# Retention and FFN on one core: output copies that step on the other side, last states on ScalarE, one q on GpSimd

## The chip, the core and the metric

The kernel runs on one core of a Trainium2 chip. The core has a matrix engine (TensorE, PE in the profile; its weight loads are shown apart as PEld), VectorE (DVE), ScalarE (ACT), GpSimd (POOL) and SyncE (SP), which here only starts DMAs. Each engine works through its own instructions in order. Products land in PSUM, which ACT and DVE read; everything else lies in SBUF. The metric is the device time of one execution in microseconds.

## What is computed

The reference is a retention layer (attention without a softmax, with a decay per head) whose output goes through a two-layer FFN with ELU. Eight batches, eight heads, 576 tokens, 64 values a head; the FFN goes from 512 to 2048 and back.

```
scores = q @ k^T / sqrt(64)                      # per batch and head, 576 x 576
gamma  = 1 - 2 ** (-5 - head)
ret    = scores * (gamma ** (i - j) if i >= j else 0)
x      = (ret @ v), heads side by side           # 4608 tokens x 512
h      = x @ w_in                                # 512 -> 2048
g      = h if h > 0 else exp(h) - 1
out    = g @ w_out                               # 2048 -> 512, float32
```

## The kernel before

The decay is separable, so q is scaled by gamma to the power of the token's position and k by its inverse (lines 224 to 235). Retention then runs in chunks: products within a chunk under a triangular mask, and a running state (the sum of k times v so far) that earlier chunks hand on.

The work is cut into **units**. Unit u is a batch b, a half T of the first 512 tokens and a half w of the heads; four units make a batch, so units 0 to 3 are the first batch and units 4 to 11 the next two (from batch 3 on, "fine" units of another shape are used). The last 64 tokens of each batch, the "riders", are worked off beside later units. For every unit the kernel

- scales and casts q and k and casts v (`cast`, with a letter per operand for the engine: v is VectorE, s ScalarE, p GpSimd),
- turns q and k over (on PE with `turn_pe` or `turn0`, later by a transposing DMA with `turn`),
- makes scores (`scores`), masks them on DVE (`masks`), multiplies them with v (`values`) and adds what earlier chunks contribute (`inter`),
- makes its own state (`state`), which DVE adds into running sums (`prefix_mid`, `prefix_end`); `put_mid` and `put_end` copy these as bf16 to where PE reads them. For the second half of a batch `put_end` calls `put_last`, which fills `s_last`; only the batch's rider reads that,
- copies the unit's output from PSUM into `xt`, the FFN's input (`put_x`, lines 392 to 403).

Tokens do not lie in order. A load gives each partition two neighbouring tokens (four for q of the first batch), so that the columns of a unit's output in PSUM come as e groups of r columns, e being 4 in the first batch and 2 in units 4 to 11. In `xt` the tokens are in order, so that the token with number r*e + i comes from column i*n + r, n being the columns of a group. `put_x` undoes this while it copies, one copy of 128 x 256 for each of the two PSUM banks `x0` and `x1`. Unit 3 is copied in two parts of 128 x 128 a bank, one of the four on DVE. Fine units copy without a step on line 398. The two banks hold one unit's output at a time: the products of the next unit must wait until the copies have read them.

The FFN's first layer (`ffn1`, and `ffn1_half` for half a batch's tokens) multiplies `xt` with `w_in`; ELU takes two ACT instructions (lines 639 and 642) and one DVE instruction (line 643); the second layer (`ffn2`) multiplies with `w_out`, and ACT copies the result for the store (line 686).

The order of all instructions on each engine is written out by hand at the end of the kernel: first the first batch's attention (lines 788 to 883), in which the weights are also loaded and cast; the FFN of the first batch with units 4 to 7 between (lines 911 to 1004); then stages that mix the FFN of one batch with the attention of the next. The loads wait in SP's queue in the order of lines 788 to 797 and 911 to 917. Products of the first FFN columns (`part`) are interleaved with unit 3's attention (lines 863 to 883). Within the span that the change touches, the order is

```
    cast(4, "p", "p", None)
    cast_w(14)
    cast_w(15)
    put_end(2)
    put_end(3)
    half1 = f1h(1, 0)
```

then a part of the second layer, the turn of unit 4 on PE, `cast_v(4, "s")`, the casts of unit 5 (line 961), more of the second layer, and `stretch(4, "p")`, which makes unit 4's scores and state and, for later units, also finishes the unit before.

Of the kernel before, what the change touches and what calls it, by code (L numbers as in the profile page):

```python
# [17 lines left out]
def kernel(  # L18
# [15 lines left out]
    P = 128  # L34
# [130 lines left out]
    def weights(k):  # L165
        for h in range(2 * (k < 2)):

            r, c = slice(2 * h * P, 2 * (h + 1) * P), slice(k * 2 * P, (k + 1) * 2 * P)
            yield h, moe_w_in[r, c].rearrange("(j p) c -> p j c", j=2), w_in_sb[:, 2 * h : 2 * h + 2, c]
        for i in (2 * k, 2 * k + 1) if k > 1 else ():  # L170
            n, j = divmod(i, KJ)
            if n < KJ:
                c = slice(n * 512, (n + 1) * 512)
                yield i % 2, moe_w_in[j * P : (j + 1) * P, c], w_in_sb[:, j, c]
            else:
                f = i - KJ * KJ
                yield i % 2, moe_w_out[f * P : (f + 1) * P, :], w_out_sb[:, f, :]

    def load_w(k):
        staged[k] = raw.tile([P, 2, 4, 2, D], FP32, name="rqk", tag="rqk").rearrange("p i h e d -> p i (h e d)")  # L180
        for h, src, dst in weights(k):
            pin(nc.sync.dma_start(staged[k][:, h] if k > 1 else staged[k][:, h].rearrange("p (j c) -> p j c", j=2), src))
# [12 lines left out]
    def fine(u):  # L195
        return seq[u][0] >= 3
# [5 lines left out]
    xps, begun = [None, None], set()  # L202

    def load(u, last=False):
        b, T, w = seq[u]
        rqk = raw.tile([P, 2, 4, 2, D], FP32, name="rqk", tag="rqk")
        rv = raw.tile([P, 4, 2, D], FP32, name="rv", tag="rv", bufs=5)
        parts = [(rqk[:, 0], q), (rqk[:, 1], k), (rv, v)]
        if fine(u):
            t = u % 4  # L210
            for dst, src in parts:
                pin(nc.sync.dma_start(
                    dst.rearrange("p a e d -> p (a e) d"), src[b, :, t * P : (t + 1) * P, :].rearrange("h p d -> p h d"),
                ))
            rawt[u] = rqk, rv
            return
        for dst, src in parts[::-1] if last else parts:
            pin(nc.sync.dma_start(
                dst.rearrange("p h e d -> p h (e d)"),
                src[b, 4 * w : 4 * w + 4, 2 * P * T : 2 * P * (T + 1), :].rearrange("h (p e) d -> p h (e d)", e=2),  # L220
            ))
        rawt[u] = rqk, rv

    def cast_qk(u, i, eng, es=(0, 1)):
        b, T, w = seq[u]
        if fine(u):
            pin(tt[eng](  # L227
                natt[u][0][:, i].rearrange("p e h d -> p (e h) d"), rawt[u][0][:, i].rearrange("p a e d -> p (a e) d"),
                (gqf, gkf)[i][:, u % 4].unsqueeze(2).to_broadcast([P, H, D]), ALU.mult,
            ))  # L230
            return
        x = rawt[u][0][:, i].rearrange("p h e d -> p e h d")
        g = (gq, gk)[i][:, 2 * T : 2 * T + 2, 4 * w : 4 * w + 4].unsqueeze(3).to_broadcast([P, 2, 4, D])
        for e in es:
            pin(tt[eng](natt[u][0][:, i, e], x[:, e], g[:, e], ALU.mult))

    def cast_v(u, eng):
        pin(engines[eng](natt[u][1], rawt[u][1]))  # L238

    def cast(u, q="p", k="p", v="p"):  # L240
        if u >= NS:
            return
        qkn = nat.tile([P, 2, 2, 4, D], BF16, name="qkn", tag="qkn")
        vn = nat.tile([P, 4, 2, D], BF16, name="vn", tag="vn", bufs=5)
        natt[u] = qkn, vn
        if q:
            cast_qk(u, 0, q)
        if k:
            cast_qk(u, 1, k)
        if v:  # L250
            cast_v(u, v)
# [43 lines left out]
    def new_x():  # L295
        for c in range(2):
            xps[c] = ps_x.tile([P, 512], FP32, name="x", tag=f"x{c}")
        begun.clear()
# [60 lines left out]
    def inter(u, hls=(0, 1), to=None):  # L359
        b, T, w = seq[u]  # L360
        x = to or xps
        if fine(u):
            for m, i, c in fines:
                if u % 4 + c:
                    r = half(c)
                    q = trt[u][r, m, r] if i == c else swapped[u][r, m]
                    acc_x(c, i, x[c][half(i), m * C : (m + 1) * C], s_fine[u % 2][r, m, i], q)
            return
        for c in range(2):
            if T + c == 0:  # L370
                continue
            s = s_mid[w] if c else s_first[w]
            for hl in hls:
                acc_x(c, 2, grouped(u, x[c][:, hl * P : (hl + 1) * P]), s[:, hl], queries(u, slice(0, P), hl, c), to)
# [17 lines left out]
    def put_x(u, hls=(0, 1), to=None, eng="ss"):  # L392
        b, T, w = seq[u]
        h0, h1 = hls[0], hls[-1] + 1
        for c in range(2):
            if fine(u):
                o = w * P + c * C
                pin(engines[eng[c]](xt_tile(b)[:, T, :, o : o + C], xps[c][:, : HP * C].rearrange("p (m n) -> p m n", m=HP)))  # L398
                continue
            e = 2 if u >= FT else 4  # L400
            src = (to or xps)[c][:, : 2 * P].rearrange("p (h e r) -> p h e r", h=2, e=e)[:, h0:h1]
            dst = xt_tile(b)[:, T, 2 * w + h0 : 2 * w + h1, c * P : (c + 1) * P].rearrange("p h (r e) -> p h e r", e=e)
            pin(engines[eng[c]](dst, src))  # L403

    def drop(u):
# [80 lines left out]
    def blocks(dst, src, eng):  # L486
        for i in range(2):
            pin(engines[eng](dst[half(i), :, half(i)], src[half(i)]))  # L488

    def put_last(b, w, src, eng):  # L490
        for i in range(2):
            pin(engines[eng](s_last[b % 3][half(w), :, i], src[half(i)]))
# [4 lines left out]
    def put_end(u, eng="p"):  # L497
        b, T, w = seq[u]
        if T:
            put_last(b, w, total[w], eng)  # L500
        else:
            blocks(s_first[w], total[w], eng)
# [32 lines left out]
    def scores_rider(b):  # L535
        for m, c, i in quads:
            t = trr[b][half(i), 2 * c + m]
            acc_x(i, c, beside(i, m, half(c)), t[:, ST:], t[:, :ST])
# [14 lines left out]
    def inter_rider(b):  # L553
        for m, c, i in quads:
            r = half(c)
            q = trr[b][r, 2 * c + m, :ST] if i == c else swapped[b, "r"][r, m]
            acc_x(c, i, beside(c, m, half(i)), s_last[b % 3][r, m, i], q)

    def values_rider(b):
        for m, c, i in quads:  # L560
            acc_x(c, i, beside(c, m, half(i)), natr[b][1][half(c), 2 * m + i], ptr[b][half(c), i, m])
# [9 lines left out]
    def stretch(u, put="p", end="p"):  # L571
        old = u - 1 in natt and u - 1 in ptt
        rider = late.pop() if late else None
        new_x()
        if rider is not None:
            inter_rider(rider)
        if old:
            inter(u - 1)
        if u < NS:
            scores(u)  # L580
            if fine(u):
                state(u)
            masks(u)
        if u in rides:
            scores_rider(rides[u])
        if old:
            values(u - 1)
        if rider is not None:
            values_rider(rider)
        if u < NS and not fine(u):  # L590
            state(u)
        if old:
            put_x(u - 1)
            drop(u - 1)
        if rider is not None:
            put_rider(rider)
        if u < NS:
            if fine(u):
                prefix_fine(u)
            else:  # L600
                prefix_mid(u, put)
                prefix_end(u, end)
        if u in rides:
            masks_rider(rides[u])
            late.append(rides[u])
# [16 lines left out]
    def xt_tile(g):  # L622
        if g == B:
            return xtail
        if g not in xts:
            xts[g] = xpool.tile([P, 2, KJ, 2 * P], BF16, name="xt", tag="xt")
        return xts[g]
# [283 lines left out]
    for kk in (4, 5, 10, 11, 6, 7, 12, 13):  # L911
        load_w(kk)
    load(4)
    for kk in (14, 15):
        load_w(kk)
    for u in range(5, 10):
        load(u)
    F = {0: {}, 1: dict(pool=ps_h, tag="ph"), 2: dict(pool=ps_h, tag="ph"), 3: {}}

    def row(ft):  # L920
# [22 lines left out]
    cast(4, "p", "p", None)  # L943
    cast_w(14)
    cast_w(15)
    put_end(2)
    put_end(3)
    half1 = f1h(1, 0)

    def some():  # L950
# [7 lines left out]
    quad(0)  # L958
    turn_pe(4, "vs", pool=ps_x, tags=("x0", "x1"))
    cast_v(4, "s")  # L960
    cast(5, "v", "p", None)
    quad(1)
    quad(2)
    stretch(4, "p")
# [5 lines left out]
    cast_v(5, "s")  # L970
    cast(6, "v", "p", None)
    quad(3)
    stretch(5, end=None)
    quad(4)
    turn_pe(6, "vs")
    cast_v(6, "s")
    cast(7, "v", "p", None)
    put_end(5)
    turn(7)
    load(10)  # L980
    quad(5)
# [77 lines left out]
    c = [j for g, hf in twos[E:] for j in f2(g, (2 * hf, 2 * hf + 1))]  # L1059
# [56 lines left out]
```

## Time and profile before

| | us |
|---|---|
| median of 3 runs | 303.45 (303.23 to 303.67) |
| profiled execution, whole | 304.17 |
| its span on the core | 302.2 |
| PE busy | 290.1 |
| ACT busy | 213.0 |
| DVE busy | 176.4 |
| POOL busy | 175.1 |

The granted clock of PE was at full speed throughout. In the rows that follow, a row of the timeline gives start and duration in microseconds, the engine, the line of the kernel, the operation, the tile written and the tiles read with their shapes, how many such instructions the row merges, and in brackets how long the engine stood idle before it and whose end released it. A row of a line's summary gives the smallest, median and largest duration in nanoseconds, then the first and last start. A row of a table by stretches gives the stretch, its length, the busy time and number of products, the granted clock, the DMA share and GB/s.

### The profile page before, as it was taken

The numbers are of one execution on the slowest core, as the hardware profiler recorded it, in microseconds if no ns is written. First come the engines' busy times: TensorE is split into PE (matmuls) and PEld (weight loads), VectorE is DVE, ScalarE is ACT, GpSimd is POOL, SyncE is SP. The second block draws the span as 40 slices with busy tenths as digits, with TensorE's granted clock in tenths as the row PEclk, the third lists the DMA queues.
The fourth block names the chain that finished last, engine by engine and source line by source line (L and its number), as shares of the span: only waits on it lengthen the run. The fifth ranks groups of instructions, "written<-read, shape, count | busy, mean of one in ns | idle before, by whom it ended". The sixth has DMA issues, their size and how long they took to land.

```text
span 302.2 us, 9051 instructions
## 1 busy us (share of the span) xinstructions
PE 290.1 (96%) x3591; PEld 176.5 (58%) x3628; DVE 176.4 (58%) x353; ACT 213.0 (70%) x433; POOL 175.1 (58%) x346
## 2 busy tenths in 40 slices
PE   8789999999999999999999999999999999999995
PEld 5444446776776666666767765554445444456654
DVE  5656568755555666756686765758675734332210
ACT  5679847976767776777777787777777776764531
POOL 7589887687957585868496887468852300011000
PEclk9999999999999999999999999999999999999999
DMA  6999999999999999999799999999761000001112
GB/s 202 316 370 356 346 304 280 227 217 172 248 177 219 169 216 235 206 207 186 191 196 215 184 199 206 202 242 177 172 90 38 37 35 36 37 35 69 37 69 69
DMA packets 132394, 54.33 MB, mean 180 GB/s; under 512 B 107712, under 2 KB 126400, under 8 KB 132352
## 3 DMA queue, kind: packets, MB, share of 16 engines
q1 hardware_dynamic: 129600, 45.04, 74.0%
q0 software_dynamic: 2672, 8.65, 8.6%
q8 instruction: 28, 0.46, 0.7%
q14 instruction: 14, 0.11, 0.1%
q10 hardware_dynamic: 80, 0.07, 0.1%
HBM read 36.70 MB, written 9.44 MB: 153 GB/s over the span
## 4 chain that ended last, share of the span: by engine, by line
PE 89%; DMA 2%; ACT 2%; issue 2%; SPq 1%; POOL 1%; DVE 1%; DVEq 0%; POOLq 0%
PE ph L65 40%; PE pm L65 39%; PE x L65 4%; PE sc L65 3%; DMA rqk<-in_k_dram 2%; PE pe L65 1%; ACT ph L642 1%; POOL s_pair L488 1%; ACT e L639 1%; SPq L731 1%; SPq L717 1%; PE ptr L269 0%; POOL qkn L750 0%; DVE pt L348 0%; DVE pt L354 0%
## 5 line engine op out<-in xcount | busy, mean ns | idle before, releaser
L643 DVE SCALAR_TENSOR_TENSOR g<-e,ph 128x512 bf16<-128x512 f32 x128 | 86.4, 686 | 84.6 <-ACT ph L642 81.2
L65 PE MATMUL ph<-xt,w_in_sb 128*128 128x256 bf16 (+1 forms) x768 | 128.7, 308 | 0.5 <-ACT xt L403 0.3
L65 PE MATMUL pm<-w_out_sb,g 128*128 128x512 bf16 x478 | 123.8, 379 | 3.1 <-issue 2.1
L639 ACT ACTIVATE e<-ph 128x512 f32<-128x512 f32 x144 | 86.0, 597 | 52.8 <-PE ph L65 51.0
L65 PEld LDWEIGHTS <-w_in_sb 128*128 128x128 bf16 x896 | 86.4, 98 | 50.7 <-issue 0.9
L642 ACT ACTIVATE ph<-ph 128x512 f32<-128x512 f32 x144 | 83.8, 591 | 0.0
L65 PEld LDWEIGHTS <-g 128*128 128x128 bf16 x512 | 48.6, 98 | 43.9 <-issue 0.2
L696 POOL DMA_DIRECT2D out_dram<-ot x35 | 19.9, 569 | 44.6 <-ACT ot L686 44.2
L468 POOL CAST s_fine<-run 64x256 bf16<-64x256 f32 x40 | 15.9, 396 | 42.4 <-DVE run L437 33.5
L686 ACT COPY ot<-pm 128x512 f32<-128x512 f32 x35 | 20.5, 588 | 14.9 <-PE pm L65 14.8
L643 DVE SCALAR_TENSOR_TENSOR gt<-e,ph 128x512 bf16<-128x512 f32 x16 | 10.9, 686 | 18.8 <-ACT ph L642 17.2
L227 POOL TENSOR_TENSOR qkn<-rqk,gqf 128x512 bf16<-128x512 f32 x20 | 21.1, 1053 | 0.4
L227 POOL TENSOR_TENSOR qkn<-rqk,gkf 128x512 bf16<-128x512 f32 x20 | 20.9, 1046 | 0.0
L65 PE MATMUL ph<-xtail,w_in_sb 128*128 128x256 bf16 x128 | 16.4, 273 | 0.0
L398 ACT CAST xt<-x 128x256 bf16<-128x256 f32 x40 | 12.9, 378 | 5.0 <-PE x L65 5.0
L437 DVE TENSOR_TENSOR run<-sc,run 128x256 f32<-128x256 f32 x35 | 14.9, 425 | 1.2
L238 POOL CAST vn<-rv 128x512 bf16<-128x512 f32 x24 | 14.6, 608 | 1.5
L341 DVE TENSOR_TENSOR pt<-sc,mask_t 128x512 bf16<-128x512 f32 x20 | 13.7, 684 | 0.0
L488 POOL CAST s_pair<-mid 64x128 bf16<-64x128 f32 x24 | 7.0, 292 | 11.4 <-DVE mid L437 6.6
L474 POOL CAST s_fine<-run 64x256 bf16<-64x256 f32 x30 | 11.9, 395 | 1.8
L459 DVE COPY qs<-qkT 64x256 bf16<-64x256 bf16 x40 | 12.0, 300 | 0.6
L65 PE MATMUL sc<-qkT 64*64 64x64 bf16 (+1 forms) x512 | 11.6, 204 | 0.5 <-ACT qkT L760 0.4
(106 smaller groups left out, 270.2 us busy)
## 6 DMA issues: line engine op xcount, KB each, us to landing
rqk<-in_q_dram SPq DMA_DIRECT2D x32, 256.0 KB, 4.3
rqk<-in_k_dram SPq DMA_DIRECT2D x32, 256.0 KB, 5.4
rv<-in_v_dram SPq DMA_DIRECT2D x32, 256.0 KB, 5.5
out_dram<-ot POOLq DMA_DIRECT2D x31, 256.0 KB, 3.4
rqk<-in_moe_w_in_dram SPq DMA_DIRECT2D x16, 256.0 KB, 5.7
rqk<-in_moe_w_out_dram SPq DMA_DIRECT2D x16, 256.0 KB, 5.9
rqt<-in_q_dram SPq DMA_DIRECT2D x8, 128.0 KB, 5.2
rqt<-in_k_dram SPq DMA_DIRECT2D x8, 128.0 KB, 4.5
```

Of the source, the lines that this page charges most:

```text
L65: pin(nc.tensor.matmul(*a, **kw))
L227: pin(tt[eng](natt[u][0][:, i].rearrange("p e h d -> p (e h) d"), rawt[u][0][:, i].rearrange("p a e d -> p (a e) d"), (gqf, gkf)[i][:, u % ...
L238: pin(engines[eng](natt[u][1], rawt[u][1]))
L341: pin(nc.vector.tensor_tensor(ptt[u], sc[:, :, : HP * C].rearrange("p i (m n) -> p i m n", m=HP), mask_t.unsqueeze(1).unsqueeze(1).to_broa ...
L398: pin(engines[eng[c]](xt_tile(b)[:, T, :, o : o + C], xps[c][:, : HP * C].rearrange("p (m n) -> p m n", m=HP)))
L437: pin(nc.vector.tensor_tensor(dst, a, b, ALU.add))
L468: pin(nc.gpsimd.tensor_copy(s_fine[u % 2][half(1), :, i], new[half(i), 0]))
L639: pin(nc.scalar.activation(e, ph, AF.Exp))
L642: pin(nc.scalar.activation(ph, ph, AF.Relu))
L643: pin(nc.vector.scalar_tensor_tensor(dst, view(e), -1.0, view(ph), ALU.add, ALU.min))
L686: pin(nc.scalar.copy(ot, pm))
L696: pin((queue or nc.gpsimd).dma_start(dst, src))
```

## The change

`put_x` reads its two sides in another order: the access pattern's inner dimension is now the group e, so that the written tokens lie side by side and the read of PSUM steps from group to group. This holds for units 0 to 11, whatever e is; fine units are untouched. `put_end(2)` and `put_end(3)` go from GpSimd to ScalarE and stand behind the cast of unit 4's v. The scaling of q of unit 5, the sixth unit, goes from VectorE to GpSimd, where the scaling of its k already was. The other lines spell out loops and default arguments and issue the same instructions in the same order.

```diff
@@ put_x
             e = 2 if u >= FT else 4
-            src = (to or xps)[c][:, : 2 * P].rearrange("p (h e r) -> p h e r", h=2, e=e)[:, h0:h1]
-            dst = xt_tile(b)[:, T, 2 * w + h0 : 2 * w + h1, c * P : (c + 1) * P].rearrange("p h (r e) -> p h e r", e=e)
+
+            src = (to or xps)[c][:, : 2 * P].rearrange("p (h e r) -> p h r e", h=2, e=e)[:, h0:h1]
+            dst = xt_tile(b)[:, T, 2 * w + h0 : 2 * w + h1, c * P : (c + 1) * P].rearrange("p h (r e) -> p h r e", e=e)
             pin(engines[eng[c]](dst, src))
@@ loads behind the first batch
-    for kk in (14, 15):
-        load_w(kk)
-    for u in range(5, 10):
-        load(u)
+    load_w(14)
+    load_w(15)
+    load(5)
+    load(6)
+    load(7)
+    load(8)
+    load(9)
@@ the first batch's FFN
     cast_w(14)
     cast_w(15)
-    put_end(2)
-    put_end(3)
     half1 = f1h(1, 0)
@@
     cast_v(4, "s")
-    cast(5, "v", "p", None)
+    put_end(2, "s")
+    put_end(3, "s")
+    cast(5, "p", "p", None)
     quad(1)
@@
-    stretch(5, end=None)
+    stretch(5, "p", end=None)
@@
-    put_end(5)
+    put_end(5, "p")
```

## The prediction

> **What bounds the kernel now.** I read the page first, then the busy time of TensorE (PE) by stretch, then the timeline of each engine around the copies that the diff touches.
>
> ```profile
> PE 290.1 (96%) x3591; PEld 176.5 (58%) x3628; DVE 176.4 (58%) x353; ACT 213.0 (70%) x433; POOL 175.1 (58%) x346
> ...
> PE 89%; DMA 2%; ACT 2%; issue 2%; SPq 1%; POOL 1%; DVE 1%; DVEq 0%; POOLq 0%
> ```
> ```profile
> 14.00:20.88 6.88, 5.40 (x150) 1.00 1.05 365
> 20.88:50.00 29.12, 28.79 (x250) 1.00 1.07 330
> ```
> PE bounds it: 96% busy, 89% of the chain that ended last. From 20.88 us on it runs almost without a gap; before, while the first batch's attention is worked off, it idles 1.48 of 6.88 us. So a change is worth what it moves of the moment at which PE starts its dense part, plus or minus new gaps later. What PE waited for ahead of 20.88:
>
> ```profile
> 15.98 0.27 PE L65 MATMUL x<-qkT,s_pair 128*128 128x128 bf16 x2 [0.39 <-POOL s_pair L488]
> ...
> 16.43 0.29 PE L65 MATMUL st<-vn,qkn 64*64 64x64 bf16 x16
> ...
> 17.42 0.24 PE L65 MATMUL x<-pt,vn 64*64 64x128 bf16 x2
> 17.98 0.41 PE L65 MATMUL x<-pt,vn 64*64 64x128 bf16 x14 [0.33 <-ACT xt L403]
> ...
> 19.23 0.23 PE L65 MATMUL st<-qkT,s_pair 128*128 128x128 bf16 x1 [0.45 <-POOL s_pair L488]
> 19.39 0.31 PE L65 MATMUL st<-pt,vn 64*64 64x128 bf16 x8
> 20.01 0.59 PE L65 MATMUL ph<-xt,w_in_sb 128*128 128x512 bf16 x2 [0.31 <-ACT xt L403]
> ...
> 20.64 0.31 PE L65 MATMUL st<-pt,vn 64*64 64x128 bf16 x8
> 20.88 1.47 PE L65 MATMUL ph<-xt,w_in_sb 128*128 128x512 bf16 x6
> ```
> ```profile
> 14.62 1.31 ACT L403 CAST xt<-x 128x256 bf16<-128x256 f32 x2 [0.17 <-PE x L65]
> 15.67 0.68 ACT L760 COPY qkT<-ptr 128x512 bf16<-128x512 bf16 x1
> 16.63 1.30 ACT L403 CAST xt<-x 128x256 bf16<-128x256 f32 x2 [0.28 <-PE x L65]
> 17.67 0.69 ACT L187 CAST w_in_sb<-rqk 128x512 bf16<-128x512 f32 x1
> 18.65 1.31 ACT L403 CAST xt<-x 128x256 bf16<-128x256 f32 x2 [0.29 <-PE x L65]
> ```
> Three pairs of output copies (units 0, 1, 2) take 1.31 us each on ScalarE (ACT). Two PE waits name them: values of unit 2 at 17.98 (unit 1's pair frees the banks at 17.93) and the first FFN product at 20.01 (unit 2's pair ends at 19.96). The wait at 15.98 names GpSimd (POOL), whose last step ahead of it ended at 15.32 + 0.62 = 15.94. But unit 0's pair ended at 15.93 too, and the weights of that product, which are the state that POOL wrote, were already loaded at 15.37:
>
> ```profile
> 15.37 0.10 PEld L65 LDWEIGHTS <-s_pair 128*128 128x128 bf16 x1
> ```
> ```profile
> 15.32 0.62 POOL L488 CAST s_pair<-end 64x128 bf16<-64x128 f32 x2
> ...
> 17.17 0.64 POOL L488 CAST s_pair<-mid 64x128 bf16<-64x128 f32 x2 [0.56 <-DVE mid L437]
> 17.87 0.62 POOL L488 CAST s_pair<-end 64x128 bf16<-64x128 f32 x2
> 18.55 0.62 POOL L488 CAST s_pair<-mid 64x128 bf16<-64x128 f32 x2
> ```
> What was missing was the bank that it writes, and unit 0's pair holds that. So all three pairs gate PE.
>
> **The output copies.** The edit swaps the stepped side for all units 0 to 11, not the first batch alone: bf16 is written contiguously, fp32 is read from PSUM in steps of 32 elements (first batch) or 64.
>
> ```profile
> L403 ACT CAST xt<-x x22: 447/462/840, 14.6 to 92.5; 128x256 bf16<-128x256 f32 x22
> ```
> ```profile
> L398 ACT CAST xt<-x x40: 372/378/389, 101.5 to 242.2; 128x256 bf16<-128x256 f32 x40
> ```
> ```profile
> 108.10 0.65 ACT L398 CAST xt<-x 128x256 bf16<-128x256 f32 x2 [0.60 <-PE x L65]
> ```
> All three rows move 128x256 from PSUM, read contiguously. Written in runs (L398): 378 ns, a pair 0.65. Written every second element (16 of the 22): about 462. Written every fourth (the other six): up to 840, a pair 1.31. So the price sits on the written side and grows with its step. No row reads PSUM in steps. Below, nothing can beat 0.65 a pair, contiguous on both sides; above, I take 1.31, as if reading in steps cost what writing every fourth did. I choose 0.65 to 0.77, near L398: the writes become L398's, and what steps now are 4-byte words read, not 2-byte ones written.
>
> [...]
>
> With 0.65 a pair, step by step:
>
> 1. Unit 0's pair ends at 15.27, so the product at 15.98 runs as soon as the transposes ahead are through, by about 15.5, and the states of unit 2 (16.43) move to about 15.95.
> 2. VectorE (DVE) cannot use all of that:
>
> ```profile
> 15.31 1.22 DVE L348 TENSOR_TENSOR pt<-sc,mask_q 128x1024 bf16<-128x1024 f32 x1 [0.20 <-PE sc L65]
> 16.82 0.29 DVE L437 TENSOR_TENSOR mid<-st,end 128x128 f32<-128x128 f32 x1 [0.28 <-PE st L65]
> ```
> Its mask runs to 16.53, so the prefix moves from 16.82 to 16.55: 0.27 earlier. POOL's three state copies (17.17 to 19.17) are back to back behind it and end at 18.90; the products at 19.23 and 19.39 move to 18.95 and 19.11.
> 3. Unit 1's pair ends before 17.42, so the fourteen products at 17.98 follow the two at 17.42 without the gap, 0.56 earlier. Unit 2's pair starts at about 18.1 and ends at 18.75, not 19.96.
> 4. The FFN product at 20.01 then waits for nothing of ACT. It comes behind the values of unit 3: eight such products hold PE for 20.88 - 20.64 = 0.24, so 19.11 + 0.24 = 19.35. That is 0.65 earlier, and the rest of the stage, its copies shorter too, follows in PE's order. **Sum: -0.65 us.**
>
> It survives a dearer read: at 1.1 a pair unit 0's ends 0.21 earlier, unit 1's 0.41, unit 2's at 18.24 + 1.1 = 19.34, still about 0.6 gained; at 1.2 half, at 1.31 nothing.
>
> Units 4 to 11 gain at most 0.12 a pair, on an ACT that PE does not wait for there: 0.
>
> **Last states on ACT.** Four 64x128 copies leave POOL (1.67 us at 41.54) and run behind ACT's cast of v:
>
> ```profile
> 41.62 0.62 ACT L238 CAST vn<-rv 128x512 bf16<-128x512 f32 x1
> 44.95 1.07 ACT L686 COPY ot<-pm 128x512 f32<-128x512 f32 x2 [2.71 <-PE pm L65]
> ```
> ```profile
> L448 ACT COPY mid<-st x2: 272/272/272, 11.5 to 14.2; 128x128 f32<-128x128 f32 x2
> ```
> By the nearest row, 0.27 each, they take 1.1 of the 2.71 us in which ACT idles. Cost 0; without that cover 1.1. Their reader, the first rider, belongs to the stretch of unit 14.
>
> **q of unit 5 on POOL.**
>
> ```profile
> 41.54 1.67 POOL L492 CAST s_last<-end 64x128 bf16<-64x128 f32 x4
> 43.28 1.19 POOL L235 TENSOR_TENSOR qkn<-rqk,gk 128x256 bf16<-128x256 f32 x2
> ```
> ```profile
> 41.86 0.85 DVE L235 TENSOR_TENSOR qkn<-rqk,gq 128x256 bf16<-128x256 f32 x2 [0.32 <-DMA rqk<-in_q_dram]
> ```
> ```profile
> 45.12 0.61 PE L269 MATMUL ptr<-ident,qkn 128*128 128x128 bf16 x8
> ```
> q lands at 41.86. On POOL it takes 1.19 (the row of k), to 43.05, and k behind it to 44.24, against 44.47 before. PE turns the unit at 45.12, or 44.47 with the shift: k is there by 0.23 us. DVE saves 0.85 of idle time. Cost 0. The two edits belong together: with the state copies still on POOL, both casts behind them would end near 43.21 + 2 x 1.19 = 45.6 and stall PE. The loads are only spelled out: 0.
>
> The sum is made on the profiled execution: 302.2 us of span, 304.17 in all, 0.72 above the median of 303.45. Taken off the median: **302.80**.
>
> **Rivals.**
>
> [...]
>
> *Half the gain: POOL really released the product at 15.98.* Then step 2 falls away, values of unit 3 stay at 19.39, the FFN starts at 19.63: -0.38, 303.07. For it: the profile names POOL, 10 ns apart. Against: the early weight load. [...]
>
> *Given back at the loads.* If k of unit 5 takes 0.5 longer on POOL, PE waits 0.3 at its turn: 303.1.
>
> **How the numbers follow.** Forecast 302.8: chance 0.56. Half or given back, 303.0 to 303.3: 0.2. Slower, 303.6 to 304.8: 0.2. More than summed: 0.04. The likeliest case alone spans 302.4 to 303.0. Range 302.2 to 304.2: it takes in the halves and the lower part of the slower case. The forecast lies just past 0.2% (0.61 us, about what a measurement of this kernel can tell from no change), so part of its chance falls within: faster 0.46, same 0.31, slower 0.23.
>
> **What would show it.** After: pairs at L403 of 0.65 to 0.77 in all 26 copies; the product of unit 1 at about 15.5; the first FFN product near 19.35 with no wait for ACT, the dense part from about 20.2; k of unit 5 done by 44.3; no PE wait at 45, 51.5 or 62. Wrong if the pairs stay above 1.1, if the start moves and the end does not, or if PE waits for POOL at unit 5's turn.

## The result, and the profile after

| | us |
|---|---|
| before, 11 runs | 303.67 median (303.15 to 304.42) |
| changed, 11 runs | 302.89 median (302.27 to 303.12) |
| ratio | 0.9962, 95% interval 0.9948 to 0.9976 |
| profiled execution of the changed kernel | 302.86, span 301.1 (before 304.17 and 302.2) |

The kernel became faster, by 0.24% to 0.52%; forecast were 0.65 us, 0.21%. (The ratio is given as recorded; the quotient of the two medians is 0.9974, or 0.78 us.) The page and the table by stretches of the changed kernel follow; this table has the busy time and the number of instructions of PE, PEld, DVE, ACT and POOL in turn, then the columns as before:

```profile
PE 292.9 (97%) x3628; PEld 176.7 (59%) x3628; DVE 176.0 (58%) x351; ACT 211.6 (70%) x437; POOL 175.7 (58%) x344
...
PE 90%; DMA 2%; ACT 2%; SPq 1%; issue 1%; POOL 1%; DVE 1%; POOLq 0%
```
```profile
14.00:19.83 5.83, 4.77 (x149) 3.06 (x141) 4.55 (x9) 3.50 (x11) 5.10 (x14) 1.00 1.06 366
19.83:49.00 29.17, 29.16 (x249) 14.40 (x246) 17.90 (x31) 23.63 (x48) 25.00 (x47) 1.00 1.11 338
```

The dense part of PE starts at 19.83, not 20.88. That is 1.05 us, and the span is 1.1 shorter: what is won there stays to the end. (PE's busy time cannot be compared: 3591 of its 3628 products are recorded before.) The copies, line 404 now: first the line's summary, then the three pairs of the first batch on the timeline of ACT:

```profile
L404 ACT CAST xt<-x x22: 372/378/395, 14.3 to 91.6; 128x256 bf16<-128x256 f32 x22
L404 ACT CAST xt<-st x3: 266/266/272, 19.0 to 19.9; 128x128 bf16<-128x128 f32 x3
...
L404 DVE CAST xt<-st x1: 291/291/291, 20.0 to 20.0; 128x128 bf16<-128x128 f32 x1
```
```profile
14.29 0.65 ACT L404 CAST xt<-x 128x256 bf16<-128x256 f32 x2 [0.17 <-PE x L65]
...
15.78 0.65 ACT L404 CAST xt<-x 128x256 bf16<-128x256 f32 x2
...
17.59 0.65 ACT L404 CAST xt<-x 128x256 bf16<-128x256 f32 x2 [0.64 <-PE x L65]
```

The 22 copies of 128x256 take 372 to 395 ns, 378 in the median, whether they step by 32 or by 64 elements in PSUM: the price of line 398, which steps on neither side. The pair is 0.65. DVE's copy of unit 3 took 444 ns in the kernel before:

```profile
L403 DVE CAST xt<-st x1: 444/444/444, 21.0 to 21.0; 128x128 bf16<-128x128 f32 x1
```

What PE makes of it:

```profile
15.10 0.27 PE L65 MATMUL x<-qkT,s_pair 128*128 128x128 bf16 x2
...
16.94 0.40 PE L65 MATMUL x<-pt,vn 64*64 64x128 bf16 x16
...
18.54 0.23 PE L65 MATMUL st<-qkT,s_pair 128*128 128x128 bf16 x1 [0.46 <-POOL s_pair L489]
18.70 0.31 PE L65 MATMUL st<-pt,vn 64*64 64x128 bf16 x8
18.94 0.60 PE L65 MATMUL ph<-xt,w_in_sb 128*128 128x512 bf16 x2
```
```profile
11.80 1.19 POOL L751 TENSOR_TENSOR qkn<-rqk,gk 128x256 bf16<-128x256 f32 x2 [1.63 <-DMA rqk<-in_k_dram]
...
14.99 0.63 POOL L489 CAST s_pair<-end 64x128 bf16<-64x128 f32 x2
...
16.47 0.64 POOL L489 CAST s_pair<-mid 64x128 bf16<-64x128 f32 x2 [0.18 <-DVE mid L438]
17.18 0.63 POOL L489 CAST s_pair<-end 64x128 bf16<-64x128 f32 x2
17.86 0.63 POOL L489 CAST s_pair<-mid 64x128 bf16<-64x128 f32 x2
```
```profile
14.99 1.23 DVE L348 TENSOR_TENSOR pt<-sc,mask_q 128x1024 bf16<-128x1024 f32 x1 [0.21 <-PE sc L65]
16.13 0.28 DVE L438 TENSOR_TENSOR mid<-st,end 128x128 f32<-128x128 f32 x1
```

The product of unit 1 runs at 15.10, in the middle of the POOL copy of 14.99 to 15.62. So that copy, which the profile of before named, does not release it; that the bank does is shown by a run below (`not_unit0`). The sixteen values at 16.94 run as one group, and the first FFN product waits for nothing.

Not all of the 1.05 is the change's. POOL could begin to scale unit 2's k at 11.80 here, at 12.13 before, ahead of everything that differs: the load came 0.33 earlier. From that point to the first FFN product it is 7.88 us before (12.13 to 20.01) and 7.14 after (11.80 to 18.94). This distance, called **the start** below, does not depend on when the loads come. It fell by 0.74.

### The profile page after: what moved, and what is told of

Read it like the earlier page. It is cut to its first block, busy times and chain, and to the rows that moved or that the text cites. A ratio compares the mean times of both kernels' runs of the same rounds, so it can differ in the third digit from the quotient of the medians.

```text
span 301.1 us, 9088 instructions
## 1 busy us (share of the span) xinstructions
PE 292.9 (97%) x3628; PEld 176.7 (59%) x3628; DVE 176.0 (58%) x351; ACT 211.6 (70%) x437; POOL 175.7 (58%) x344
## 4 chain that ended last, share of the span: by engine, by line
PE 90%; DMA 2%; ACT 2%; SPq 1%; issue 1%; POOL 1%; DVE 1%; POOLq 0%
PE pm L65 40%; PE ph L65 40%; PE x L65 5%; PE sc L65 3%; DMA rqk<-in_k_dram 2%; PE pe L65 1%; POOL s_pair L489 1%; ACT ph L643 1%; ACT e L640 1%; SPq L732 1%; SPq L718 1%; PE ptr L269 0%; DVE pt L348 0%; PE st L65 0%; POOL qkn L751 0%
## 5 line engine op out<-in xcount | busy, mean ns | idle before, releaser
L65 PE MATMUL pm<-w_out_sb,g 128*128 128x512 bf16 x512 | 129.6, 379 | 0.0
```

Source lines behind the costliest of these rows:

```text
L65: pin(nc.tensor.matmul(*a, **kw))
```

## The experiments

The first series of runs undid or kept parts of the change. The new sides of the copies alone (`x_alone`):

```diff
@@ kernel before
-            src = (to or xps)[c][:, : 2 * P].rearrange("p (h e r) -> p h e r", h=2, e=e)[:, h0:h1]
+            src = (to or xps)[c][:, : 2 * P].rearrange("p (h e r) -> p h r e", h=2, e=e)[:, h0:h1]
...
```

> The kernel before with the two rearranged sides of the output copies alone. Measure of the start: from the first of GpSimd's two scalings of unit 2's k (the end of its wait for the DMA) to the first FFN product: 7.88 us before (12.13 to 20.01), 7.14 after (11.80 to 18.94). If the copies are the whole cause: 7.14, and a ratio of 0.996 to 0.999 to the kernel before. If the moved casts and copies of states carry part of the gain: the start still 7.14, but a time nearer to the kernel before.

The changed kernel with the old sides, that is the moved states and q alone (`rest_alone`):

> The changed kernel with the old sides of the output copies, so the last states on ScalarE and q of unit 5 on GpSimd alone. If the copies are the whole cause: start 7.88, ratio 1.000 within 0.15%. If these moves free something that PE waits for: below 0.999 with a start of 7.88, the gain lying behind 40 us.

The new sides for units 0 to 3 alone (`first_batch`) and for 4 to 11 alone (`later_units`), by `if u < FT` or `if u >= FT` in both lines:

> The kernel before with the new sides for units 0 to 3 alone. If only the first batch's copies gate PE: start 7.14 and the same ratio as with all twelve units. If units 4 to 11 count too (pairs of 0.77 against 0.65): less than that by up to 0.12 us a pair.

> The kernel before with the new sides for units 4 to 11 alone. If only the first batch's copies gate PE: start 7.88, ratio 1.000 within 0.15%, pairs of 0.65 behind 46 us. If the later copies count: up to 0.3 us faster.

The second series:

```diff
@@ changed kernel: not_unit0 (old sides where u is 0)
+            ... "p (h e r) -> p h r e" if u > 0 else "p (h e r) -> p h e r" ...
@@ changed kernel: q_states_pool
     cast_w(15)
+    put_end(2)
+    put_end(3)
...
-    put_end(2, "s")
-    put_end(3, "s")
@@ changed kernel: end1_act
-    put_end(1)
+    put_end(1, "s")
```

> The changed kernel with the old sides for unit 0's two copies alone (a pair of 1.31 instead of 0.65). If unit 0's copies release the product of unit 1 (bank, not GpSimd's state): that product starts 3.85 us behind the first scaling of unit 2's k (3.30 in the changed kernel), GpSimd's three state copies move back 0.36, and the start is 7.50 us. If GpSimd's state copy releases it: the start stays 7.14.

> The changed kernel with the last states back on GpSimd, ahead of the cast of unit 5's q, which also stays there. By the prediction's sum (copies of 1.67 us, then two casts of 1.19) k of unit 5 ends so late that PE waits 0.5 to 1.2 us at the turn of unit 5 and the time is that much above the changed kernel. Rival: the 1.67 were stretched by VectorE's cast beside them; alone they take about 1.2, k ends 0.4 us ahead of the turn, and the time is the changed kernel's.

> The changed kernel with the end state of unit 1 copied by ScalarE in place of GpSimd. If the start is now bound by GpSimd's three state copies in a row (16.47 to 18.49, the product at 18.54 waits 0.46 for them): the third starts right behind VectorE's prefix, 0.3 us earlier, and the start is 6.85, the ratio to the kernel before 0.001 lower than the changed kernel's. If something else binds it (the mask of unit 3 on VectorE): the start stays 7.14.

> The kernel before once more. In the two profiles so far unit 2's k arrives at 12.13 us (before) and 11.80 (after), ahead of everything that the change touches. If that is chance: it arrives somewhere between 11.7 and 12.3 in all these runs without regard to the kernel, and the start is 7.88 us here. If it belongs to the kernel: near 12.13 in every kernel with the old casts and near 11.80 in the changed ones. Ratio 1.000.

The third series repeated three kernels beside one new one, the changed kernel with `cast(5, "v", "p", None)`, so q of unit 5 on DVE again (`x_states_act`):

> The changed kernel once more, beside the next three. Theory now: the copies bring 0.72 us at the start; the moved states and q keep it, since k of unit 5 is cast right behind the last weights and not behind the state copies. So start 7.14, no wait of PE at the turn of unit 5 (the turn begins 23.17 us behind the first ELU and its eight products start within 0.39), ratio near 0.9965. Rival: the moves do nothing, and the first comparison's 0.9962 was chance; then the ratio is that of the copies alone.

> The copies alone once more. Theory: start 7.14 to 7.21, but k of unit 5 ends some 2.9 us behind the last weights' cast, and PE waits 0.3 to 0.65 at the turn of unit 5 (0.30 in the first profile of it); ratio 0.998, between the kernel before and the changed one. Rival (the moves do nothing): the ratio of the changed kernel.

> The changed kernel with q of unit 5 back on VectorE: the copies and the states on ScalarE. If taking the states out of GpSimd's queue is what keeps the gain: no wait at the turn of unit 5, and the changed kernel's ratio. If q on GpSimd matters too (VectorE's cast stretches GpSimd's beside it, as the state copies of 0.42 instead of 0.30 each suggest): k takes 1.4 instead of 1.19 and PE waits up to 0.2.

> The changed kernel with unit 1's end state on ScalarE, once more: start 6.85, the ratio 0.001 below the changed kernel's of the same call. If the loads now bind (k of unit 5 lands too late for the earlier start), PE waits 0.1 to 0.3 at the turn of unit 5 and the two are the same within 0.05%.

What was measured. The ratio is to the kernel before in the same series. "k" is when POOL begins with unit 2's k, "start" the distance from there to the first FFN product, and "turn" by how much later than in the kernel before PE is through with the turn of unit 5, counted from the end of the products ahead of it; these three are from the one profile of each run.

| kernel | ratio (95%) | k | start | turn |
|---|---|---|---|---|
| before | 1 | 12.13 | 7.88 | 0 |
| before_again | 0.9998 (0.9982 to 1.0014) | 12.34 | 7.89 | 0.61 |
| later_units | 1.0005 (0.9990 to 1.0019) | 11.56 | 7.88 | 0 |
| rest_alone | 0.9996 (0.9969 to 1.0023) | 11.40 | 7.87 | 0 |
| changed | 0.9962 (0.9948 to 0.9976) | 11.80 | 7.14 | 0 |
| after_again | 0.9970 (0.9953 to 0.9987) | 11.43 | 7.13 | 0 |
| x_alone | 0.9984 (0.9966 to 1.0002) | 11.90 | 7.21 | 0.30 |
| x_alone_2 | 0.9974 (0.9954 to 0.9994) | 11.76 | 7.13 | 0.86 |
| first_batch | 0.9996 (0.9982 to 1.0011) | 11.09 | 7.12 | 0.65 |
| x_states_act | 0.9969 (0.9946 to 0.9991) | 11.92 | 7.21 | 1.02 |
| q_states_pool | 1.0001 (0.9987 to 1.0016) | 11.19 | 7.15 | 0.78 |
| not_unit0 | 0.9981 (0.9966 to 0.9996) | 11.69 | 7.50 | 0 |
| end1_act | 0.9943 (0.9929 to 0.9958) | 11.68 | 6.85 | 0.10 |
| end1_act_2 | 0.9947 (0.9927 to 0.9966) | 11.60 | 6.85 | 0 |

**The start belongs to the first batch's copies.** Every kernel with old copies there has 7.87 to 7.89, every one with new ones 7.12 to 7.21, whatever later moves it holds; `end1_act`, which changes the start itself, comes below. The later units' copies change nothing. POOL begins with k between 11.09 and 12.34 without regard to the kernel, so the 0.33 of the first pair of profiles is within this spread and not the change's. (In thirteen profiles POOL waits for the load there, until 12.13 at the latest; in `before_again` the profile names ACT's copy of `mid`.) In `not_unit0` the two copies of unit 0 have their old sides again:

```profile
14.17 1.31 ACT L404 CAST xt<-x 128x256 bf16<-128x256 f32 x2 [0.17 <-PE x L65]
```
```profile
14.87 0.62 POOL L489 CAST s_pair<-end 64x128 bf16<-64x128 f32 x2
```
```profile
15.53 0.27 PE L65 MATMUL x<-qkT,s_pair 128*128 128x128 bf16 x2 [0.39 <-POOL s_pair L489]
...
19.18 0.60 PE L65 MATMUL ph<-xt,w_in_sb 128*128 128x512 bf16 x2
```

The pair ends at 15.48 and the product follows at 15.53, 3.84 behind k's 11.69. POOL's copy ends at 15.49, so the bracket names it again; but it ends 3.8 behind k in the changed kernel too (15.62), where the product did not wait for it. Only the pair moved, and the product with it. The start is 7.50, as expected to the hundredth. So half of the gain, 0.36, comes by unit 0's pair, DVE's prefix and POOL's three copies. The other half is left to the pairs of units 1 and 2, which no run told apart.

**The loads blur the times.** `first_batch` has the whole gain at the start and shows none in its ratio, where that of all twelve units was expected; its profile loses 0.65 again at the turn. `after_again` has the gain and lost 1.21 us once:

```profile
29.20 0.59 PE L65 MATMUL pm<-w_out_sb,g 128*128 128x512 bf16 x2 [1.21 <-POOL w_out_sb L187]
```
```profile
27.86 0.62 POOL L187 CAST w_in_sb<-rqk 128x512 bf16<-128x512 f32 x1 [1.61 <-DMA rqk<-in_moe_w_in_dram]
28.53 2.65 POOL L187 CAST w_out_sb<-rqk 128x512 bf16<-128x512 f32 x4
```

A weight came late, POOL waited 1.61 for it, and PE waited for the cast behind it. Such waits differ from execution to execution: PE waits for a cast of `w_out_sb` 0.5 us in the profile of `x_states_act`, 0.4 in `q_states_pool`, 0.2 in `before_again`, and not in the others. That an earlier start brings PE closer to them is likely, but not shown. In the one profile of `rest_alone` it is not a load but the granted clock (the column of 0.57), behind its first FFN product:

```profile
19.00:23.00 4.00, 3.73 (x18) 0.57 1.04 363
```

From the first FFN product to the first of the second layer, PE takes 6.35 us there (19.27 to 25.62) against 4.76 in the kernel before (20.01 to 24.77), so 1.59 are lost.

**The turn of unit 5.** Expected was, in the third series, that the states' leaving POOL's queue keeps the gain. `x_states_act` speaks against it: the states are on ACT, and the wait is the longest of all.

```profile
43.33 0.76 DVE L235 TENSOR_TENSOR qkn<-rqk,gq 128x256 bf16<-128x256 f32 x2 [2.04 <-DMA rqk<-in_q_dram]
44.01 1.22 DVE L348 TENSOR_TENSOR pt<-sc,mask 128x1024 bf16<-128x1024 f32 x1
...
45.55 0.29 DVE L438 TENSOR_TENSOR end<-x,mid 128x128 f32<-128x128 f32 x1
```
```profile
44.15 1.19 POOL L235 TENSOR_TENSOR qkn<-rqk,gk 128x256 bf16<-128x256 f32 x2 [1.05 <-DMA rqk<-in_k_dram]
```
```profile
42.51 0.42 PE L65 MATMUL sc<-qkT 64*64 64x128 bf16 x16
45.90 0.61 PE L269 MATMUL ptr<-ident,qkn 128*128 128x128 bf16 x8 [1.01 <-DVE end L438]
```

PE made unit 4's scores at 42.51. DVE stood 2.04 us ahead of the cast of q, whose load was late, and the mask of unit 4 is queued behind it. Mask, prefix, end state follow one another to 45.84, and PE turns unit 5 at 45.90: the turn's first product writes bank x1, which holds unit 4's state until DVE has read it. k was done at 45.34, so it is not k. `x_alone_2` shows the same with less delay; its wait of 0.86 is longer than the 0.3 to 0.65 expected, and comes from DVE and not, as expected, from k:

```profile
42.32 0.85 DVE L235 TENSOR_TENSOR qkn<-rqk,gq 128x256 bf16<-128x256 f32 x2 [1.79 <-DMA rqk<-in_q_dram]
43.09 1.21 DVE L348 TENSOR_TENSOR pt<-sc,mask 128x1024 bf16<-128x1024 f32 x1
...
44.64 0.29 DVE L437 TENSOR_TENSOR end<-x,mid 128x128 f32<-128x128 f32 x1
```
```profile
44.98 0.61 PE L269 MATMUL ptr<-ident,qkn 128*128 128x128 bf16 x8 [0.86 <-DVE end L437]
```

In the kernel before, q is done at 42.71, ahead of the scores, and DVE waits for these:

```profile
43.23 1.22 DVE L348 TENSOR_TENSOR pt<-sc,mask 128x1024 bf16<-128x1024 f32 x1 [0.51 <-PE sc L65]
```

In the changed kernel q is not in DVE's queue. DVE waits for the scores, not for a load, and the turn follows the products ahead of it without a wait:

```profile
42.17 1.23 DVE L348 TENSOR_TENSOR pt<-sc,mask 128x1024 bf16<-128x1024 f32 x1 [1.69 <-PE sc L65]
43.73 0.29 DVE L438 TENSOR_TENSOR end<-x,mid 128x128 f32<-128x128 f32 x1
```
```profile
44.07 0.61 PE L269 MATMUL ptr<-ident,qkn 128*128 128x128 bf16 x8
```

In all five profiles that wait with q on DVE the turn begins 0.05 to 0.06 behind the end state on DVE. How late q comes differs, so the sizes of these waits cannot be compared as they stand. Counted from the first FFN product, q's cast begins 24.20 us later in `x_states_act`, and the one profile with q on POOL that is as late, `after_again` (24.17), had lost 1.21 us of PE ahead of the turn. At like times the place of q does count: with q on DVE, PE waits 0.30 when the cast begins 22.76 us later (`x_alone`) and 0.65 at 23.12 (`first_batch`); with q on POOL and the states on ACT, nothing at 22.63 (`end1_act_2`) and 0.10 at 23.18 (`end1_act`). These are one profile each, of kernels that differ elsewhere too.

With q on POOL but the states there too, it is k after all (`q_states_pool`):

```profile
41.37 1.32 POOL L493 CAST s_last<-end 64x128 bf16<-64x128 f32 x4
42.77 1.18 POOL L235 TENSOR_TENSOR qkn<-rqk,gq 128x256 bf16<-128x256 f32 x2
43.91 1.18 POOL L235 TENSOR_TENSOR qkn<-rqk,gk 128x256 bf16<-128x256 f32 x2
```
```profile
45.15 0.29 PE L269 MATMUL ptr<-ident,qkn 128*128 128x128 bf16 x2 [0.28 <-POOL qkn L235]
```

The last two of the eight products wait for k, done at 45.09. The turn is over 0.78 later, and the time is that of the kernel before: the gain is given back. So in the profiles the two moves guard it together: q leaves the queue that the mask stands in, and the states make room for q on POOL. How often the wait comes up in executions without a profile was not measured, and the ratios of one series (`after_again` 0.9970, `x_alone_2` 0.9974, `x_states_act` 0.9969) cannot tell the three kernels apart. That the moves shorten the time is therefore not shown.

**A faster version.** With the copies short, POOL's three state copies bind the start. `end1_act` gives the middle one to ACT, which had 0.64 us idle:

```profile
16.10 0.61 ACT L489 CAST s_pair<-end 64x128 bf16<-64x128 f32 x2
```
```profile
17.38 0.62 POOL L489 CAST s_pair<-mid 64x128 bf16<-64x128 f32 x2 [0.47 <-DVE mid L438]
```
```profile
18.06 0.23 PE L65 MATMUL st<-qkT,s_pair 128*128 128x128 bf16 x1 [0.47 <-POOL s_pair L489]
18.22 0.31 PE L65 MATMUL st<-pt,vn 64*64 64x128 bf16 x8
18.45 0.60 PE L65 MATMUL ph<-xt,w_in_sb 128*128 128x512 bf16 x2
```

In `end1_act_2` the third copy runs right behind DVE's prefix; the start is 6.85, as expected. It is faster than the kernel before in both series (0.9943 and 0.9947). Beside the changed kernel in the same series (0.9970) its median is 0.97 us lower, 302.68 against 303.65, though the two intervals overlap. Expected was a ratio lower by 0.001, and it is lower by 0.0023. The start accounts for 0.28 us; what the rest is stays open.

## Why the prediction was right, and where its sum was off

- **The price of the stepped read**, on which the sign hung: right at its lower end, 0.65 a pair. The 1.31 a pair taken as its upper end is out: 378 ns with every element 128 or 256 bytes from the last within a group, and DVE's copy fell from 444 to 291 ns. (The 462 that the prediction gives for every second element is the median of all 22 copies; the sixteen have 447 to 472, in the median 452.) No run shows the loss that the slower case, 303.6 to 304.8, was an estimate of: the pairs of units 4 to 11, 0.76 to 0.78 us in the kernel before (50.53, 57.37, 61.00), take 0.64 to 0.66 in the changed one (49.60, 56.44, 60.08), and `later_units`, with the stepped read for these units alone, has a ratio of 1.0005.
- **Who releases the product of unit 1:** right, the bank. It moved from 3.85 to 3.30 behind k, and `not_unit0` put it back to 3.84.
- **Steps 1 to 4:** the chain was as written, its sum of 0.65 was 0.74. The term that was too small is step 2: the mask was let run to its end, 16.53, before the prefix starts. On DVE the prefix starts at 16.13 while the row of the mask lasts to 16.22, so DVE and, behind it, POOL moved by 0.36 and not 0.27. That is the missing 0.09.
- **Last states on ACT:** four copies took 1.22 us by ACT's row (1.1 forecast) and are hidden: ACT then waits 1.59 us for PE.
- **q on POOL at cost 0:** no cost, but the reason given, idle DVE time, missed what is queued behind q. Before, q ends at 42.71 on DVE and the mask behind it starts at 43.23, with the scores: a slack of 0.52, less than the shift of 0.74. The prediction counted k's slack on POOL and not this one. With q left on DVE, the shift alone would have met it, and did: 0.30 in the first profile of `x_alone`, where q begins at 41.87 (41.86 before). That both moves belong together was right as far as the profiles go: k, put "near 45.6" with the states on POOL, was done at 45.09 in `q_states_pool`, and PE lost 0.78.
- **Given back at the loads** did not happen in the first profile: k of unit 5 is done at 42.89, well ahead of the turn at 44.07, and PE has no new wait near 51.5 or 62, in the first layer's products behind the copies of units 5 and 7, either. Another load did cost `after_again` 1.21 us; whether the earlier start had a part in that is not shown.
- **The size:** the start gives 0.74 us, 0.24%, against the 0.21% forecast, and the medians differ by 0.78 us (0.65 in the third series). By the ratio (0.38%, its interval from 0.24%) there may be more than the start. That could be waits at the turn that the kernel before has in some executions (0.61 in `before_again`); no run shows it.

## What to carry to other kernels

Where a copy out of PSUM must reorder elements, try letting it step on the read and write 2-byte elements in runs: here, with fp32 read and bf16 written by ACT, this halved a pair of copies from 1.31 to 0.65 us where the writes had stepped by four. A copy on an engine with idle time can still be on the path: ACT was busy 70% of the span, and yet PE stood 0.33 and 0.31 us (at 17.98 and 20.01 in the kernel before) until ACT's pairs had read the banks and filled `xt`. Look at the weight load of a product that waits: here it had run at 15.37, the product came at 15.98, and what was missing was not the weights but the bank (`not_unit0`). And when the path gets shorter, look at what stands in a queue behind an instruction that waits for a load: its slack was measured against the old start, here 0.52 us against a shift of 0.74.

## What was not expected of the hardware

Writing bf16 every fourth element cost up to 840 ns against 378 for 128x256, on ACT, while reading fp32 from PSUM every 32nd or 64th cost nothing that shows (372 to 395 ns over 22 copies). The same load came up to 1.04 us apart (11.09 to 12.13) in the thirteen profiles in which POOL waits for it, more than the whole gain. And the granted clock was 0.57 on average from 19 to 23 us in one of fourteen profiles (`rest_alone`), whose mean over the span is 0.994 against 0.998 or more in the others.
